# Fewer weight units decoded under attention, raw tiles behind the gates' rows, one gate and val step in two parts

## The chip, the cores and the metric

The kernel runs on one core of one Trainium2 chip. The metric is the device time of one execution in microseconds (us). A profiled execution has a span besides, from its first to its last instruction.

## The reference, cut to what matters

```python
# attention, 2 x 8 heads, 576 positions, 64 dims (8 "pairs" of heads in the kernel)
scores = scale * q @ k.T ; cum = cumsum(max(s, 0))
scores = where(causal, -1e9, scores + min(-(cum_i - cum_j), 0))   # the gates' rows carry cum
x = softmax(scores) @ v                     # [1152, 512]
xn = x / sqrt(mean(x*x) + 1e-6) * rms_g
g, val = xn @ w_gate, xn @ w_val            # [1152, 1536]; the "gate and val" steps
y = (silu(g) * val) @ w_out                 # [1152, 512]
h = y @ w_in ; out = (h * tanh(log(1 + exp(h)))) @ w_out2
```

All inputs arrive as float32 but for the weights, which arrive as 64-bit words.

## The kernel before

Attention runs over eight pairs of heads (p = 0 to 7). A pair has five score units, so there are 40 units, numbered i = 5p + u, and the order of the program is written out by hand: every operation is an event `at(t, f, ...)` whose time t is counted in units, and the events are sorted by t. Each engine and each DMA queue then works through its own instructions in that order, and waits at its head for what the instruction needs.

For pair p+1 the events of pair p load four things. `load_k` and `load_q` (L120, L123, 576 KB each) are issued by POOL at i + 0.2. `load_raw` (L116, two halves of 288 KB, one per head) goes at i + 0.3, on ACT's queue for p below 3 and on SP's from p = 3 on. `load_cum` (L128, L129, four small DMAs of the gates' rows) goes on SP at i + 1.47, and `load_v` (L144) at i + 3.58. Then `q_lo` (L140) and `k_lo` (L134) subtract the rounded q and k from the raw ones: those of the first head on POOL at i + 3.14 and i + 3.28, those of the second on VectorE (DVE) at i + 4.19 and i + 4.89. The first score unit of pair p+1 (PE L391, L392) needs the first head's two.

The weights are 68 units of 512 KB. A unit is loaded by `w_load` (L298) into a tile r and decoded in steps: `w_a` (ACT, L310), `w_b` (two DVE operations, L315 and L317), `w_c` (a copy on ACT, L326, and a subtraction, L328, on POOL during attention and on DVE afterwards). The next load into the same tile waits for the subtraction, and the SP queue is held meanwhile. With `NA = 8` the events decode one unit per pair: `wa` at i + 5.21, `wb` at i + 8.38 and 8.46, `wc` at i + 10.45. So units 0 to 6 are decoded by the end of attention and unit 7 is begun. The first two loads are on ACT's queue, at the times `lim1` (2.19) and `lim8` (8.49). The rest is decoded by `w_tick`, whose event times for the head of the second stage are the list `T["tk"]`; a tick finds the next unit by itself.

After attention comes the head of the second stage, at `to` = 43.83. There `gate_val(0, 0)` to `gate_val(0, 3)` (PE L591, 24 matmuls each, the first twelve with gate weights and the last twelve with val weights) run while the second half of x is normed: `xn_sq` (ACT L516), twelve small DVE operations (`rs_op`, L521 to L531), `xn_scale_t` (ACT L544, five tiles), and the transposes `xn_1` (PE L549). A gate and val step takes one of two PSUM tiles, which `silu` (ACT L598, DVE L599) gives back.

Much later, in the loop over the 36 `y_acc` steps (PE L622), a tick follows each odd k, k = 23 among them, where `y_evac` (L629, L630) also stands. `h_split` (ACT L604, DVE L605) makes the input of the step two ahead.

Of the kernel before, what the change touches and what calls it, by code (L numbers as in the profile page):

```python
# [27 lines left out]
NP = B * H // 2  # L28
# [3 lines left out]
NF, NF2 = DFF // 128, DFF2 // 128  # L32
TB = 384
NB = NTOK // TB
NA = 8
NPRE = 4
KD = DM // 128
KW = 2 * S
# [4 lines left out]
def tile_kernel(ctx: ExitStack, tc: tile.TileContext, kq, qq, v, s, w1, w2, rms_g, out):  # L43
    nc = tc.nc
# [199 lines left out]
    def unit(n):  # L244

        if n < NI:
            return ring_unit(n % 8)
        if n < NU1:
            return w14_unit(n - NI)
        n -= NU1  # L250
        if n < 9:
            return ring_unit((n + 8) % 9)
        if n < 15:
            return slot_unit((0, 5)[n % 2 == 0], (n - 9) // 2)
        if n < 27:
            return w14_unit(n - 15)
        return slot_unit((7, 11)[n // 3 - 9], n % 3)


    gv_done, y_done = set(), set()  # L260
# [74 lines left out]
    def w_tick():  # L335

        n = done["c"]
        if n >= NUW or not free(seq[n]):
            return
        w_loads(LIM[0])  # L340
        done["t"] += 1
        for m in range(done["a"], min(n + 3, done["l"])):
            if m > n and done["t"] - loaded[m] < AGE:
                break
            w_a(m)
            done["a"] = m + 1
        for m in range(done["b"], min(n + 2, done["a"])):
            w_b(m)
            done["b"] = m + 1
        if n < done["b"]:  # L350
            w_c(n)
            done["c"] = n + 1
        w_loads(LIM[0])
# [208 lines left out]
    def banksS():  # L562
        return psS[1].tile([128, 2, 512], F32, tag="S", name="gv")
# [9 lines left out]
    gv_t, h_t, y_t, htile = {}, {}, {}, {}  # L573
# [6 lines left out]
            htile[z] = sbt([128, 8, TB], F32, n, f"h_{n}")  # L580
        return htile[z][:, y]

    def gate_val(b, f):
        t = banksS()
        gv_t[b, f] = t
        for g in range(2):
            n = 0
            w = unit(2 * f + g)
            for c in range(KD):
                for a, r in PASS:  # L590
                    nc.tensor.matmul(t[:, g, 0:TB], w[:, a, 128 * c:128 * c + 128],  # L591
                                     xhl[r][:, c, TB * b:TB * b + TB], start=(n == 0), stop=(n == 11))
                    n += 1
        gv_done.add((b, f))

    def silu(b, f):
        t, h = gv_t.pop((b, f)), h_at(b, f)
# [3 lines left out]
    def h_split(b, f):  # L601
        h = h_at(b, f)
        h_t[b, f] = hhl = sbt([128, 2, TB], F32R, ("hA", "hB", "mm")[(NF * b + f) % 3], "hhl")
        nc.scalar.copy(out=hhl[:, 0], in_=h)  # L604
        nc.vector.tensor_tensor(out=hhl[:, 1], in0=h, in1=hhl[:, 0].bitcast(F32), op=ALU.subtract)  # L605

    def y_acc(b, f):
        if f == 0:
            if b % 2:
                a0, a1 = banksS(), banksS()  # L610
                y_t[b] = [x[:, y, 0:TB] for x in (a0, a1) for y in range(2)]
            else:
                a0 = psT.tile([128, 512], F32, tag="T", name="y0")
                a1 = psT.tile([128, 512], F32, tag="T", name="y1")
                a2 = psT.tile([128, 512], F32, tag="T", name="y2")
                a3 = psX.tile([128, 512], F32, tag="X", name="y3")
                y_t[b] = [x[:, 0:TB] for x in (a0, a1, a2, a3)]
        hhl = h_t.pop((b, f))
        w = unit(NI + f)
        for d in range(KD):  # L620
            for y, (a, r) in enumerate(PASS):
                nc.tensor.matmul(y_t[b][d], w[:, a, 128 * d:128 * d + 128], hhl[:, r],  # L622
                                 start=(f == 0 and y == 0), stop=(f == NF - 1 and y == 2))
        y_done.add((b, f))

    def y_evac(b, ds=range(KD)):
        for d in ds:
            h, l = (x[:, d, TB * b:TB * b + TB] for x in xhl)
            nc.scalar.copy(out=h, in_=y_t[b][d])  # L629
            nc.vector.tensor_tensor(out=l, in0=y_t[b][d], in1=h.bitcast(F32), op=ALU.subtract)  # L630
# [209 lines left out]
    def at(t, f, *args):  # L840
        events.append((t, len(events), f, args))
# [51 lines left out]
    for p in range(NP):  # L893
        i = 5 * p
        z = "z" if p == NP - 1 else ""
        for x in range(2):
            for c, o in enumerate(T[f"av{x}{z}"]):
                at(i + o, av_op, p, x, c)
            at(i + T["xte" + z][x], xt_evac, p, x)
            at(i + T["xtr" + z][x], x_transposes, p, x)  # L900
            at(i + T["xn" + z][x], x_norm, p, x)
        at(i + T["rec" + z], recips, p)
        if NP - NA <= p:
            n = p - NP + NA
            at(i + T["wa"], wa, n)
            if p + 1 < NP:
                at(i + T["wb"][0], wb, n, 0)
                at(i + T["wb"][1], wb, n, 1)
                at(i + T["wc"], wc, n)
        if p + 1 < NP:  # L910
            q1 = nc.scalar if p < 3 else nc.sync
            if p:
                at(i + 0.3, load_raw, p + 1, q1)
                at(i + 0.2, load_k, p + 1)
                at(i + 0.2, load_q, p + 1)
            if p:
                at(i + T["lcum"], load_cum, p + 1)
            at(i + T["lv"], load_v, p + 1, q1)
            los, eng = (T["lo"], T["_le"]) if p else (T["lo0"], T["_l0"])
            for x in range(4):  # L920
                at(i + los[x], (k_lo, q_lo)[x % 2], p + 1, x // 2, nc.vector if eng[x] == "D" else nc.gpsimd)
# [10 lines left out]
    for o, n in ((1.9, 3), (2.05, 2), (3.05, 2), (3.5, 1), (3.95, 2), (4.1, 2)):  # L932
        at(o, busy_x, n)
    at(0.65, q_lo, 0, 1)
    at(T["lim1"], limit, 1, nc.scalar)
    at(T["lim8"], limit, 8, nc.scalar)
    for t in range(5):
        at(T["sq"][t], xn_sq, 0, t)
    for n in range(3):
# [8 lines left out]
    steps1 = [(0, f) for f in range(NPRE)] + [(b, f) for f in range(NPRE) for b in range(1, NB)] + \  # L948
        [(b, f) for f in range(NPRE, NF) for b in range(NB)]
    steps2 = [(b, f) for b in range(NB) for f in range(NF)]  # L950
    to = T["mlp"]
# [1 line left out]
    at(T["limN"], limit, NUW)  # L953
    K0 = len(T["gv"])
    for k in range(K0):
        at(to + T["gv"][k], gate_val, *steps1[k])
        at(to + T["silu"][k], silu, *steps1[k])
    for o in T["tk"]:
        at(to + o, w_tick)
# [12 lines left out]
    for k in range(K0, len(steps1)):  # L972
        gate_val(*steps1[k])
        silu(*steps1[k])
        if k + 1 < len(steps1):
            w_tick()
        if k + 3 >= len(steps1):
            h_split(*steps2[k + 3 - len(steps1)])
    for k, (b, f) in enumerate(steps2):
        if k:  # L980
            w = k + 2
            if w < len(steps2):
                h_split(*steps2[w])
        y_acc(b, f)
        if f == NF - 1 and b < NB - 1:
            y_evac(b)
        if k % 2 == 1:
            w_tick()
    h2_mm(0, 0)
    mlp2.append(True)  # L990
# [110 lines left out]
```

## Time and profile before

| | us |
|---|---|
| median of 3 runs | 543.95 |
| lowest and highest run | 540.23, 544.28 |
| the profiled execution | 543.94 |
| its span | 542.2 |

A PE instruction that waits inside the pipeline can count as busy, so its busy share says little by itself. What the rest of the text reads is where an engine's idle time is noted behind an instruction, in square brackets with the releaser, and which instruction followed which.

### The profile page before, as it was taken

How to read it: one execution, taken by the hardware profiler on the slowest of the kernel's cores; microseconds unless marked ns; L12 is line 12 of the kernel's file. 1: busy time of each engine (PE TensorE's matmuls, PEld its weight loads, DVE VectorE, ACT ScalarE, POOL GpSimd, SP SyncE). 2: the span in 40 equal slices, each digit the busy share in tenths (PEclk: the TensorE clock that was granted, in tenths of full speed). 3: DMA queues.
4: the chain of work that ended last, by engine and by line, in shares of the span. 5: the costliest groups of instructions: out<-in, count | busy, mean ns of one | idle time of the engine just before them, and what ended most of it. 6: DMA issues, size and time to landing. Idle time of an engine off the chain costs nothing.

```text
span 542.2 us, 8007 instructions
## 1 busy us (share of the span) xinstructions
PE 530.3 (98%) x2993; PEld 476.9 (88%) x2993; DVE 339.0 (63%) x718; ACT 265.7 (49%) x594; POOL 56.9 (10%) x67
## 2 busy tenths in 40 slices
PE   8999998999999999999999999999999999999997
PEld 3677775778999999999999999998989999999885
DVE  7989998664635544554567547487678766653321
ACT  5778996677434334433446355555424343333311
POOL 7246455110000000000000000000000000000000
PEclk9999998799999999999999999999999999999999
DMA  9997992203234344434433405344300100000101
GB/s 213 273 246 213 247 244 95 79 8 149 77 94 140 117 119 131 139 116 121 133 100 114 117 1 156 116 117 124 109 0 2 59 1 1 0 1 0 60 0 58
DMA packets 18502, 55.46 MB, mean 102 GB/s; under 512 B 2136, under 2 KB 2392, under 8 KB 18464
## 3 DMA queue, kind: packets, MB, share of 16 engines
q1 hardware_dynamic: 13536, 42.02, 25.1%
q0 software_dynamic: 3488, 9.44, 8.8%
q10 hardware_dynamic: 1440, 3.51, 2.1%
q8 instruction: 23, 0.38, 0.3%
q14 instruction: 15, 0.12, 0.1%
HBM read 52.47 MB, written 2.36 MB: 101 GB/s over the span
## 4 chain that ended last, share of the span: by engine, by line
PE 85%; ACT 6%; DVE 4%; DMA 2%; issue 1%; POOL 0%; ACTq 0%; DVEq 0%; POOLq 0%
PE gv L591 26%; PE o L696 12%; PE y L622 8%; PE gv L646 8%; PE gv L696 6%; PE gv L622 4%; PE xa L477 4%; PE pa L784 3%; PE pc L784 3%; PE pd L784 3%; PE tp L439 3%; ACT px L423 2%; DMA w<-in_qq_dram 2%; PE sc L391 1%; PE pb L784 1%
## 5 line engine op out<-in xcount | busy, mean ns | idle before, releaser
L591 PE MATMUL gv<-xh,wring 128*128 128x384 f32 x576 | 147.8, 337 | 0.0
L591 PEld LDWEIGHTS gv<-xh,wring 128*128 128x128 f32 x576 | 104.0, 188 | 0.1
L591 PE MATMUL gv<-xl,wring 128*128 128x384 f32 x288 | 96.8, 336 | 0.0
L599 DVE TENSOR_TENSOR h_w<-h_w,gv 128x384 f32<-128x384 f32 x36 | 19.9, 554 | 62.4 <-ACT h_w L598 62.4
L598 ACT ACTIVATE h_w<-gv 128x384 f32<-128x384 f32 x36 | 17.7, 491 | 79.5 <-PE gv L591 79.5
L591 PEld LDWEIGHTS gv<-xl,wring 128*128 128x128 f32 x288 | 54.2, 188 | 0.0
L622 PE MATMUL y<-hhl,w 128*128 128x384 f32 x288 | 50.5, 334 | 0.6 <-DVE hhl L605 0.6
L622 PEld LDWEIGHTS y<-hhl,w 128*128 128x128 f32 x288 | 49.9, 188 | 0.9 <-DVE hhl L605 0.9
L317 DVE SCALAR_TENSOR_TENSOR r<-r 128x512 int32<-128x512 int32 x68 | 48.2, 709 | 3.0
L423 ACT ACTIVATE px<-sc,cst 128x384 f32<-128x384 f32 (+2 forms) x80 | 41.3, 531 | 3.6 <-DVE cst L416 3.6
L310 ACT ACTIVATE r<-r 128x512 f32<-128x512 f32 x57 | 38.3, 675 | 2.7 <-DMA r<-in_w_dram 2.1
L416 DVE CUSTOM_DVE_ANT_0 sc<-sc,xtm 128x384 f32<-128x384 f32 (+4 forms) x72 | 34.7, 499 | 4.6 <-PE sc L392 3.2
L605 DVE TENSOR_TENSOR hhl<-h_w,hhl 128x384 fp32r<-128x384 f32 x36 | 19.8, 555 | 24.6 <-ACT hhl L604 24.6
L604 ACT CAST hhl<-h_w 128x384 fp32r<-128x384 f32 x36 | 18.5, 518 | 31.7 <-PE y L622 18.1
L439 PE MATMUL tp<-cst,px 128*128 128x128 f32 (+1 forms) x200 | 31.4, 287 | 2.6 <-ACT aw L458 0.9
L439 PEld LDWEIGHTS tp<-cst,px 128*128 128x128 f32 (+1 forms) x200 | 24.3, 145 | 8.1 <-ACT aw L458 1.1
L477 PE MATMUL xa<-aw,px 128*64 128x320 f32 (+3 forms) x192 | 30.2, 384 | 0.1
L315 DVE TENSOR_SCALAR r<-r 128x512 int32<-128x512 int32 x68 | 29.3, 431 | 0.0
L676 DVE TENSOR_TENSOR glb<-u,glb 128x768 fp32r<-128x768 f32 x20 | 19.1, 955 | 15.9 <-ACT glb L675 15.7
L696 PE MATMUL o<-wt,glb 128*128 128x512 f32 x108 | 26.9, 390 | 0.0
L696 PE MATMUL o<-w,glb 128*128 128x512 f32 x108 | 26.5, 390 | 0.0
L622 PE MATMUL gv<-hhl,w 128*128 128x384 f32 x144 | 25.1, 334 | 0.0
(202 smaller groups left out, 1025.7 us busy)
## 6 DMA issues: line engine op xcount, KB each, us to landing
r<-in_w_dram SPq DMA_DIRECT2D x66, 512.0 KB
w<-in_kq_dram POOLq DMA_DIRECT2D x7, 576.0 KB, 5.5
w<-in_qq_dram POOLq DMA_DIRECT2D x7, 576.0 KB, 6.4
out_dram<-osb SPq DMA_DIRECT2D x8, 256.0 KB
px<-in_v_dram SPq DMA_DIRECT2D x5, 320.0 KB
r<-in_w_dram ACTq DMA_DIRECT2D x2, 512.0 KB
px<-in_v_dram ACTq DMA_DIRECT2D x3, 320.0 KB
raw_hA<-in_kq_dram SPq DMA_DIRECT2D x3, 288.0 KB
```

Of the source, the lines that this page charges most:

```text
L310: nc.scalar.activation(out=top, in_=top, func=ACTF.Prelu, scale=2.0 ** -112, alpha=-2.0 ** 32)
L315: nc.vector.tensor_scalar(out=low, in0=low, scalar1=29, scalar2=None, op0=ALU.logical_shift_right)
L317: nc.vector.scalar_tensor_tensor(out=low, in0=top, scalar=3, in1=low, op0=ALU.logical_shift_left, op1=ALU.bitwise_or)
L416: nc.vector.tensor_tensor_reduce(out=sv, in0=sv, in1=m, scale=-0.125, scalar=first, op0=ALU.add, op1=ALU.min, accum_out=sbias[:, c:c + 1])
L423: nc.scalar.activation(out=pv, in_=sv, func=ACTF.Exp, bias=sbias[:, c + x:c + x + 1], scale=-1.0, accum_out=ssum[:, sc:sc + 1])
L439: nc.tensor.transpose(t[0:rows, o - a:o - a + 128], P[pos[i] % 2][:, o:min(e, o + 128)], ident)
L477: nc.tensor.matmul(o, V[z][0:rows, c, ds], r, start=(c == 0), stop=(c == (1, 4)[part]))
L591: nc.tensor.matmul(t[:, g, 0:TB], w[:, a, 128 * c:128 * c + 128], xhl[r][:, c, TB * b:TB * b + TB], start=(n == 0), stop=(n == 11))
L622: nc.tensor.matmul(y_t[b][d], w[:, a, 128 * d:128 * d + 128], hhl[:, r], start=(f == 0 and y == 0), stop=(f == NF - 1 and y == 2))
L646: nc.tensor.matmul(t[:, x, 0:TB], w[:, a, 128 * c:128 * c + 128], xhl[r][:, c, TB * b:TB * b + TB], start=(n == 0), stop=(n == 11))
L696: nc.tensor.matmul(o_t[b][tt], gl[:, r, x, 128 * tt:128 * tt + 128], w[:, a], start=(g == 0 and x == 0 and y == 0), stop=(g == NG - 1 and ...
L784: nc.tensor.matmul(t, A[a][:, 128 * c:128 * c + 128], B[r][:, c], start=(start and n == 0), stop=(n == 5), skip_group_check=True)
```

## The change

`NA` goes from 8 to 6: one weight unit per pair is decoded from pair 2 on instead of from pair 0 on, so units 0 to 4 are finished in attention and unit 5 is begun. The first two loads of weights move by ten units of time with it. Units 5, 6, 7 and the one after them are then decoded by the ticks that stood there before for units 7 and the one after it; two ticks that did nothing now do work. From p = 3 on `load_raw` stands behind `load_cum`. `gate_val(0, 3)` is issued in two parts: its twelve gate matmuls ahead of the transposes `xn_1(0)`, its twelve val matmuls where the whole step stood. In the loop over `y_acc` the tick of k = 23 moves behind the step k = 24.

```diff
-NA = 8
+NA = 6
-    def gate_val(b, f):
-        t = banksS()
-        gv_t[b, f] = t
-        for g in range(2):
+    def gate_val(b, f, parts=(0, 1)):
+        if 0 in parts:
+            gv_t[b, f] = banksS()
+        t = gv_t[b, f]
+        for g in parts:
             n = 0
             w = unit(2 * f + g)
...
-        gv_done.add((b, f))
+        if 1 in parts:
+            gv_done.add((b, f))
...
-                at(i + 0.3, load_raw, p + 1, q1)
+                at(i + (0.3 if p < 3 else T["lcum"] + 0.01), load_raw, p + 1, q1)
                 at(i + 0.2, load_k, p + 1)
                 at(i + 0.2, load_q, p + 1)
...
-    at(T["lim1"], limit, 1, nc.scalar)
-    at(T["lim8"], limit, 8, nc.scalar)
+    at(T["lim1"] + 5 * (NP - NA), limit, 1, nc.scalar)
+    at(T["lim8"] + 5 * (NP - NA), limit, 8, nc.scalar)
...
     for k in range(K0):
-        at(to + T["gv"][k], gate_val, *steps1[k])
+        if k == NPRE - 1:
+            at(to + T["m1"][0] - 0.01, gate_val, *steps1[k], (0,))
+            at(to + T["gv"][k], gate_val, *steps1[k], (1,))
+        else:
+            at(to + T["gv"][k], gate_val, *steps1[k])
...
-        if k % 2 == 1:
+        if k % 2 == 1 and k != 2 * NF - 1 or k == 2 * NF:
             w_tick()
```

## Rows read from the trace of the kernel before

**Rows 1.** Windows by stage: busy us of each engine, granted clock, DMA share, GB/s.
```profile
core 0: us, PE busy (x) PEld busy (x) DVE busy (x) ACT busy (x) POOL busy (x), PEclk, DMA share, GB/s
44.00:84.00 40.00, 39.64 (x290) 29.37 (x288) 37.34 (x130) 35.45 (x123) 20.86 (x18) 1.00 0.94 242
84.00:92.00 8.00, 5.88 (x40) 3.78 (x41) 7.66 (x17) 5.97 (x17) 6.02 (x6) 0.99 0.15 45
92.00:102.00 10.00, 10.00 (x42) 8.04 (x44) 7.06 (x24) 5.45 (x20) 4.01 (x5) 0.50 0.32 107
137.00:320.00 183.00, 183.00 (x1057) 183.00 (x1057) 98.72 (x183) 76.20 (x144) 0.00 (x0) 1.00 0.38 113
```

**Rows 2.** Timeline of PE (start, us, instruction, [idle before]): first scores of four pairs.
```profile
31.14 0.33 PE L391 MATMUL sc<-w 128*128 128x128 f32 x1
43.19 0.33 PE L391 MATMUL sc<-w 128*128 128x128 f32 x1 [0.50 <-POOL w L134]
65.89 0.33 PE L391 MATMUL sc<-w 128*128 128x128 f32 x1
77.11 0.33 PE L391 MATMUL sc<-w 128*128 128x128 f32 x1
```

**Rows 3.** Timeline of ACT, pair 1: one decode step.
```profile
21.63 0.68 ACT L310 ACTIVATE r<-r 128x512 f32<-128x512 f32 x1
```

**Rows 4.** Timeline of SP's queue, 52 to 72 us.
```profile
52.16 0.42 SPq L116 DMA_DIRECT2D raw_mm<-in_kq_dram  x1
57.95 0.33 SPq L298 DMA_DIRECT2D r<-in_w_dram  x1
60.02 0.47 SPq L129 DMA_DIRECT2D w<-cC  x1
71.56 0.47 SPq L129 DMA_DIRECT2D w<-cC  x1
```

**Rows 5.** Timeline of POOL, pairs 4 and 5.
```profile
62.53 1.42 POOL L140 TENSOR_TENSOR w<-raw_mm,w 64x576 fp32r<-64x576 f32 x1 [4.61 <-issue]
64.03 1.81 POOL L134 TENSOR_TENSOR w<-raw_mm,w 64x576 fp32r<-64x576 f32 x1
66.42 0.72 POOL L123 DMA_DIRECT2D w<-in_qq_dram  x1
72.60 1.88 POOL L140 TENSOR_TENSOR w<-raw_hA,w 64x576 fp32r<-64x576 f32 x1 [3.13 <-issue]
```

**Rows 6.** Timeline of DVE: second head's subtractions for pairs 5 and 6.
```profile
62.77 1.80 DVE L134 TENSOR_TENSOR w<-raw_r,w 64x576 fp32r<-64x576 f32 x1
74.43 0.75 DVE L134 TENSOR_TENSOR w<-raw_hB,w 64x576 fp32r<-64x576 f32 x1
```

**Rows 7.** Timelines of ACT's queue, POOL, SP's queue, ACT: loads, issue and landing.
```profile
20.68 0.33 ACTq L116 DMA_DIRECT2D raw_hA<-in_kq_dram  x1
27.70 1.41 POOL L140 TENSOR_TENSOR w<-raw_hA,w 64x576 fp32r<-64x576 f32 x1 [8.06 <-DMA raw_hA<-in_kq_dram]
324.57 2.93 SPq L298 DMA_DIRECT2D r<-in_w_dram  x2
328.06 0.70 ACT L310 ACTIVATE r<-r 128x512 f32<-128x512 f32 x1 [0.26 <-DMA r<-in_w_dram]
```

**Rows 8.** Timelines of ACT and DVE, head of the second stage.
```profile
121.66 0.63 ACT L516 ACTIVATE w<-w 128x512 f32<-128x512 f32 x1
124.24 0.17 DVE L521 TENSOR_SCALAR cst<-cst 128x5 f32<-128x5 f32 x1 [1.89 <-ACT w L516]
126.79 3.18 ACT L544 ACTIVATE w<-w,cst 128x512 f32<-128x512 f32 x5 [1.87 <-DVE cst L531]
126.61 0.55 DVE L599 TENSOR_TENSOR h_w<-h_w,gv 128x384 f32<-128x384 f32 x1
```

**Rows 9.** Timelines of DVE and PE around the tick of k = 23.
```profile
323.85 0.69 DVE L328 TENSOR_TENSOR wt<-r,wt 128x512 fp32r<-128x512 f32 x1
325.06 1.14 PE L622 MATMUL y<-hhl,w 128*128 128x384 f32 x5 [0.60 <-DVE hhl L605]
```

## The prediction

> **What bounds the kernel now.** I read the windows by stage first, to see where an engine has slack; then the timelines of PE, SP's queue, POOL and DVE through attention, to see what each waits for; then the head of the second stage and the place of the moved tick. In the windows [rows 1] the reader is to see three things. From 137 us on PE is busy all the time, 1057 matmuls in 183 us or 0.173 us each, with DVE and ACT about half idle: work moved there costs nothing as long as it stays off PE's path. From 44 to 84 us nobody has slack: PE 39.64 of 40 us, DVE 37.34, ACT 35.45, and the DMA engines 0.94. And from 92 to 102 us the granted clock is 0.50, the lower of the two levels (1.2 GHz), after a stretch of 8 us in which PE was busy for only 5.88 [rows 1].
>
> The starts of the pairs on PE say what a pair costs [rows 2]: 31.14 to 43.19 is 12.05 us, 43.19 to 65.89 is two pairs of 11.35, 65.89 to 77.11 is 11.22. PE notes one wait there, 0.50 us ahead of pair 3, for POOL's `k_lo` [rows 2]. So about 11.2 us is PE's own pace, and only the first pairs stand above it.
>
> **The change, part by part.** The sum is made against the profiled execution, 543.94 us, which is the median of the runs (543.95) but for 0.01.
>
> *Fewer units under the first pairs.* The chain ahead of pair 2 loses one `w_a` on ACT, 0.68 us long [rows 3], of which I count 0.5, since PE's own work comes up right behind it. Pair 3 starts after a wait of 0.50 for POOL [rows 2]; POOL loses one subtraction, and a later raw load leaves q's transfer freer. Gain 1.0. Bounds: 0, because PE may be the next limit at once, and 1.7, which is what 12.05 + 11.35 - 2 x 11.22 leaves (0.96) plus the 0.68 in pair 1. DVE's and POOL's savings in these pairs beyond that I cost at nothing: PE's pace of 11.2 covers them. Pairs 2 to 6 decode one unit each as before, only with a lower number, so nothing else changes there.
>
> *Raw tiles behind the gates' rows.* This is the part that decides. For pair 5 SP issues raw at 52.16 now, 5.8 us ahead of the weight load at 57.95, which waits for POOL's decode of the unit before; the last gates' row goes at 60.02 [rows 4]. Moved behind it, the two halves go at 60.02 + 0.47 = 60.5 and 61.0. A load of 512 KB on a DMA that is otherwise idle landed 3.5 us after its issue (324.57 to 328.06) [rows 7]. The two halves together hold 576 KB, so by that row the first is there at about 63.4 and the second at 64.0. They are wanted at 62.53 by POOL [rows 5] and at 62.77 by DVE [rows 6]: late by 0.9 and 1.2. Behind DVE's `k_lo` stand the maxima of the last score unit of pair 4, and ACT's exponentials wait for those; behind POOL's two subtractions (62.53 to 65.84 [rows 5]) stands PE's first score matmul at 65.89 [rows 2], which has 0.05 us to spare. I take 1.2. For pair 6 the last row goes at 71.56 [rows 4], so the halves land at 74.9 and 75.5, wanted at 72.60 [rows 5] and 74.43 [rows 6]: late by 2.3 on POOL, where PE has 0.6 to spare (72.60 + 1.88 and the other 1.9 end near 76.5, PE starts at 77.11), and by 1.1 on DVE. Of that the delay that pair 5 already gave is to be taken off on POOL, and I take 1.2 again. Pair 4's raw load meets no weight load ahead of it on SP, because the first two weight loads are on ACT's queue, and pair 7's meets DMA engines with a share of 0.15 [rows 1] and a POOL that has other work to do first: nothing for both. Together a loss of 2.4. Bounds: 0, if the tiles still land in time, because the transfers of k and q have the DMA engines to themselves meanwhile and are out of the way; and 5.0 a pair, 10 in all, if they take the 7.0 us that raw needed in pair 1, issued at 20.68 and awaited until 27.70 among other transfers [rows 7]. I stay near the 3.5 because k and q are issued 6 us or more ahead here (q at 66.42 for a raw load at 72.0 [rows 5]) and 2 us ahead there.
>
> Here the Trainium skill speaks against the change: "DMA: Bandwidth & Descriptors", section "Rules for kernel authors", says to issue a DMA early and wait on it late, so that its fixed cost overlaps with compute; the raw loads do so before and not after. The same page's fit in "Anatomy of one DMA" (2.0 us and the bytes at 436 GB/s) gives 3.35 us for both halves, an estimate from that page; the loss by it would be 1.05 a pair instead of 1.2.
>
> *The head of the second stage.* Two more units are decoded by ticks between the sums of squares (from 121.66) and the twelve small DVE operations (from 124.24) [rows 8]. That is four more ACT instructions of about 0.68 [rows 3], 2.7 us, and one DVE subtraction of 0.69 [rows 9] in series with the last of them: 3.4 us. So the small operations begin at 127.6, end 2.55 later (124.24 to 126.79 [rows 8]) at 130.2, and the five scalings (3.18 [rows 8]) end at 133.4 instead of 129.97. The gate half moved ahead of the transposes gives PE 12 x 0.173 = 2.1 us of work in that time. It can't start at once: it needs the PSUM tile that DVE's L599 gives back, and that stands behind the small operations (126.61 now [rows 8], 130.2 then). Loss between 0 and 3.4 - 2.1 = 1.3; I take 0.6, since the transposes, which now get their tiles one at a time, will find most of them scaled. The new loads are hidden: the tiles are free two decodes ahead, and 3.5 us [rows 7] is less than the 4 us of a gate and val step; without that cover ACT would wait for each.
>
> *The tick of k = 23.* PE waits 0.60 for DVE's L605, which stands behind that tick's decode, the last of it L328 at 323.85 [rows 9]. Moved one step later the decode is behind L605 on DVE. Gain 0.6 (bounds 0 and 0.6); next late would be the load behind the tick, by one subtraction, and its user is a tick that PE doesn't wait for within 2 us.
>
> Sum: -1.0 + 2.4 + 0.6 - 0.6 = +1.4, so 545.3 us.
>
> **The rivals.** *B, the raw loads are hidden after all*, so this part of the change does nothing: -1.0 + 0.6 - 0.6 = -1.0, 542.9 us. For it: both needs are missed by about 1 us only, and without raw k and q land sooner. Against it: DMA engines at 0.94 until 84 us [rows 1].
>
> *C, the clock doesn't fall.* The fall at 92 us follows PE's waits from 84 to 92 us [rows 1], and the order of POOL's and DVE's work there shifts when raw comes later. At the higher level (2.4 GHz) the 10.0 us of PE work would be 5.0, and DVE's 7.06 [rows 1] would be the limit: a gain of 2.9 to 5, and one of the three runs of before was 3.7 below the median. With 3.7 it gives 541.6, with B 539.2. Against it: the operations that made PE wait there are all still in the program. The Trainium skill ("TensorE: Matmul & The Clock Gate", "What's actually happening") has recent activity release the clock; the drop after 5.88 of 8 us agrees.
>
> *D, slower.* The raw tiles come late by 3 us or more per pair, because a second weight load (on ACT's queue, the moved `lim8`) travels with k and q of pair 5. At the bound of 5.0 a pair the sum is -1.0 + 10 + 0.6 - 0.6 = +9.0, 552.9 us. It decides from a landing of 5.3 us on, where two pairs lose 6.
>
> **How the numbers follow.** About 1% (5.4 us) is what a measurement of this kernel can tell from no change. The forecast, 543.9 to 548, has a chance of 0.48; B, 541.5 to 543.9, 0.22; C 0.15; D, 548 to 553, 0.15. Faster by over 1% is below 538.5: C with B and the largest early gain, 0.10. Slower by over 1% is above 549.4: the upper part of D, 0.13. The rest, 0.77, is within 1%. The range of 539.5 to 550 leaves out the ends of C and D.
>
> **What would show it.** Late raw: POOL's first L140 of pairs 5 and 6 waits for a raw tile's DMA, and so does DVE's L134; the first scores of these pairs are 12 us or more apart. Early gain: pair 3 starts without a wait, a microsecond sooner. Head: L521 starts 3 us later after the first gate matmuls than now. Tick: no wait of PE for L605. The prediction is wrong if pairs 5 and 6 keep 11.2 us (B), if the granted clock stays at 1.00 through attention (C), or if it falls a second time.

## The result, and the profile after

The changed kernel takes 547.42 us (median; 543.51 to 555.8), the kernel before 543.45 us on the same chips. The ratio is 1.0064, with an interval of 1.004 to 1.0087: slower by about 3.5 us by the ratio, and by 4.0 by the medians, inside 1%. The ratios here and below leave out the executions that lie over 1.5% above the fastest of their kernel; the medians have them in. Its profiled execution took 548.29 us, with a span of 546.5.

The windows of the changed kernel, with the columns of [rows 1]:

```profile
core 0: us, PE busy (x) PEld busy (x) DVE busy (x) ACT busy (x) POOL busy (x), PEclk, DMA share, GB/s
0.00:20.00 20.00, 17.26 (x63) 9.71 (x63) 12.68 (x34) 9.08 (x26) 12.70 (x27) 0.83 0.94 196
44.00:84.00 40.00, 38.22 (x273) 28.66 (x272) 33.90 (x107) 34.51 (x115) 17.72 (x16) 0.96 0.82 208
92.00:102.00 10.00, 9.04 (x70) 6.83 (x66) 9.69 (x27) 8.07 (x27) 7.53 (x8) 1.00 0.20 50
112.00:137.00 25.00, 22.11 (x128) 19.52 (x128) 12.38 (x35) 15.68 (x34) 2.60 (x2) 0.93 0.48 148
320.00:326.00 6.00, 6.00 (x36) 6.00 (x36) 2.11 (x4) 1.87 (x4) 0.00 (x0) 1.00 0.00 1
```

The fall of the granted clock at 92 to 102 us [rows 1] is gone (1.00), but there are three others: at the start (0.83 over the first 20 us), behind 70 us (0.96 over 40 us), and in the head (0.93 over 25 us). Everything from 44 to 84 us is a little less busy than in [rows 1]. From 320 to 326 us PE is busy throughout.

PE's timeline, first score matmuls of pairs 5 and 6, and the matmuls in the head that waited:

```profile
69.50 0.33 PE L391 MATMUL sc<-w 128*128 128x128 f32 x1 [1.74 <-POOL w L134]
82.35 0.33 PE L391 MATMUL sc<-w 128*128 128x128 f32 x1
131.34 0.44 PE L592 MATMUL gv<-xh,wring 128*128 128x384 f32 x1 [2.15 <-DVE h_w L601]
140.73 0.44 PE L592 MATMUL gv<-xh,wring 128*128 128x384 f32 x1 [0.20 <-DVE h_w L601]
143.14 0.44 PE L592 MATMUL gv<-xh,wring 128*128 128x384 f32 x1 [0.55 <-ACT xh L555]
143.94 0.44 PE L592 MATMUL gv<-xl,wring 128*128 128x384 f32 x1 [0.36 <-DVE xl L556]
```

Against [rows 2], pairs 5 and 6 start 3.61 and 5.24 us later. Pair 5 shows a wait of its own. L592 and L601 are L591 and L599 of before.

SP's queue, POOL and DVE, the raw tiles of pairs 5 and 6 (the answer to [rows 4, 5]):

```profile
61.97 0.47 SPq L129 DMA_DIRECT2D w<-cC  x1
62.49 0.40 SPq L116 DMA_DIRECT2D raw_mm<-in_kq_dram  x1
66.17 1.41 POOL L140 TENSOR_TENSOR w<-raw_mm,w 64x576 fp32r<-64x576 f32 x1 [6.29 <-DMA raw_mm<-in_kq_dram]
79.00 1.41 POOL L140 TENSOR_TENSOR w<-raw_hA,w 64x576 fp32r<-64x576 f32 x1 [5.91 <-DMA raw_hA<-in_kq_dram]
80.48 1.81 POOL L134 TENSOR_TENSOR w<-raw_hA,w 64x576 fp32r<-64x576 f32 x1
66.82 1.37 DVE L134 TENSOR_TENSOR w<-raw_r,w 64x576 fp32r<-64x576 f32 x1 [2.14 <-DMA raw_r<-in_kq_dram]
79.63 1.40 DVE L134 TENSOR_TENSOR w<-raw_hB,w 64x576 fp32r<-64x576 f32 x1 [1.14 <-DMA raw_hB<-in_kq_dram]
```

The raw load stands behind the last gates' row, and POOL now waits for it by name, in pair 5 and in pair 6 (issued at 75.70), and so does DVE for the second halves. In pair 6 POOL's L134 ends at 82.29 and PE begins at 82.35, without a wait of its own: from 71 to 74 us PE was at the lower clock and came late itself.

ACT and DVE in the head (the answer to [rows 8]):

```profile
118.32 0.68 ACT L310 ACTIVATE r<-r 128x512 f32<-128x512 f32 x1 [1.83 <-DMA r<-in_w_dram]
123.34 1.24 ACT L310 ACTIVATE r<-r 128x512 f32<-128x512 f32 x2
127.86 0.69 DVE L328 TENSOR_TENSOR w<-r,w 128x512 fp32r<-128x512 f32 x1 [1.37 <-ACT w L326]
128.47 0.16 DVE L521 TENSOR_SCALAR cst<-cst 128x5 f32<-128x5 f32 x1
130.74 0.55 DVE L601 TENSOR_TENSOR h_w<-h_w,gv 128x384 f32<-128x384 f32 x1
130.92 3.17 ACT L544 ACTIVATE w<-w,cst 128x512 f32<-128x512 f32 x5 [2.70 <-DVE cst L531]
```

Three units, 6, 7 and 8, are decoded here. The first waits 1.83 us for its load, which SP issued at 113.32 and which landed 4.9 us later. The last one's subtraction (127.86) is what the first small operation, L521, stands behind. L601, which gives the PSUM tile back, stands behind the last of the small ones, and PE waits for it at 131.34.

To compare the traces below, I cut each at three places of PE's timeline: from the first matmul of pair 1 (before it the starts differ by up to 4 us) to the first gate matmul, "pairs"; from there to the gate step (1, 0), "head"; from there to the end of the span, "rest".

| trace | units in attention | raw of pairs 4; 5 to 7 | fourth gate | pairs | head | rest | granted clock falls, from pair 1 on |
|---|---|---|---|---|---|---|---|
| before | 8 | early | whole | 95.99 | 21.30 | 405.41 | 92 to 102 |
| after | 6 | late | two parts | 93.45 | 24.62 | 405.77 | 71 to 74, 132 to 136 |
| e2_raw_only | 8 | late | whole | 95.86 | 21.29 | 405.31 | none |
| e5_tick_only | 8 | early | whole | 91.11 | 21.30 | 404.55 | none |
| e12_eight_units | 8 | late | two parts | 96.10 | 20.63 | 406.01 | 72 to 75 |
| e7_gate_whole | 6 | late | whole | 94.31 | 27.62 | 404.33 | 67 to 74, 132 to 139 |
| e10_raw_between | 6 | between; early | two parts | 91.68 | 21.95 | 405.76 | none |

The stretches of before add to 522.70 and those of after to 523.84; the rest of the spans' difference, 3.16 us, lies ahead of pair 1, where the granted clock was 0.83 over the first 20 us in the profile of after and 1.00 in that of before.

The table has one profile of each kernel, and the granted clock differs between executions of one kernel too. It is on record for each execution as a mean. Of the 85 counted executions of the kernel before beside the experiments, the seven with a mean of 1.000 took 539.7 to 540.5 us, and the six with 0.984 took 545.1 to 547.2: some 4 us for 0.01. Over all 85 the mean is 0.992, and over the 19 counted ones of the changed kernel it is 0.992 too. So falls of the clock move a single profile by more than most of the differences below, but they don't account for the 3.5 us by which the changed kernel is slower.

### The profile page after: what moved, and what is told of

Read it like the earlier page. It is cut to its first block, busy times and chain, and to the rows that moved or that the text cites. A ratio compares the mean times of both kernels' runs of the same rounds, so it can differ in the third digit from the quotient of the medians.

```text
span 546.5 us, 7996 instructions
## 1 busy us (share of the span) xinstructions
PE 531.1 (97%) x2993; PEld 478.2 (87%) x2993; DVE 339.1 (62%) x720; ACT 266.9 (49%) x594; POOL 53.1 (10%) x65
## 4 chain that ended last, share of the span: by engine, by line
PE 82%; DVE 5%; DMA 5%; issue 3%; ACT 2%; POOL 1%; SPq 1%; ACTq 0%; DVEq 0%; POOLq 0%
PE gv L592 25%; PE o L698 12%; PE y L624 9%; PE gv L648 8%; PE gv L698 6%; PE gv L624 5%; PE pa L786 3%; PE pc L786 3%; PE pd L786 3%; PE tp L439 2%; DMA raw_hB<-in_kq_dram 2%; PE xa L477 2%; PE pb L786 1%; PE sc L391 1%; DMA w<-in_qq_dram 1%
## 5 line engine op out<-in xcount | busy, mean ns | idle before, releaser
L592 PE MATMUL gv<-xh,wring 128*128 128x384 f32 x576 | 149.2, 339 | 2.9 <-DVE h_w L601 2.4
L592 PEld LDWEIGHTS gv<-xh,wring 128*128 128x128 f32 x576 | 104.9, 189 | 3.8 <-DVE h_w L601 2.8
L592 PE MATMUL gv<-xl,wring 128*128 128x384 f32 x288 | 97.3, 338 | 0.4 <-DVE xl L556 0.4
L601 DVE TENSOR_TENSOR h_w<-h_w,gv 128x384 f32<-128x384 f32 x36 | 19.9, 553 | 62.4 <-ACT h_w L600 62.4
L592 PEld LDWEIGHTS gv<-xl,wring 128*128 128x128 f32 x288 | 54.4, 189 | 0.6 <-DVE xl L556 0.6
L391 PE MATMUL sc<-w 128*128 128x384 f32 (+1 forms) x64 | 24.3, 390 | 1.8 <-POOL w L134 1.7
```

Source lines behind the costliest of these rows:

```text
L391: nc.tensor.matmul(o, QA[z][:, qs], KA[z][:, ks], start=(n != 1), stop=False)
```

## The experiments

Theory L: the raw tiles come late from pair 5 on, and the two more units lengthen the head; the lighter first pairs and the tick give back less. Its rivals are told with each run.

**The raw tiles early again, in the changed kernel.**

```diff
-                at(i + (0.3 if p < 3 else T["lcum"] + 0.01), load_raw, p + 1, q1)
+                at(i + 0.3, load_raw, p + 1, q1)
```

> The changed kernel with one part undone: load_raw stands again ahead of the gates' rows (i + 0.3 for every pair). Theory L (the late raw tiles cost about 1.7 us at pair 5 and 1.6 us at pair 6, as the profile of the changed kernel has 12.94 and 12.85 us there against 11.2): about 3.3 us less than the changed kernel, some 544 us, ratio to before near 1.000; pairs 5 and 6 start 11.2 to 11.5 us apart, and POOL's L140 no longer waits for a raw tile in pairs 4 to 7. Rival W (the two weight loads that now travel in pairs 2 and 3 on ACT's queue make the tiles late): the intervals stay near 12.9 and the time near 547. Rival H (the head of the second stage holds all of the loss): 547 as well, with the intervals short.

549.05 us, ratio 1.0135 (1.009 to 1.0181): slower than the changed kernel, where a gain was expected. PE's first matmul of pair 3, POOL, and SP's queue:

```profile
33.77 0.72 POOL L123 DMA_DIRECT2D w<-in_qq_dram  x1
33.76 0.33 SPq L116 DMA_DIRECT2D raw_hA<-in_kq_dram  x1
46.14 1.96 POOL L140 TENSOR_TENSOR w<-raw_mm,w 64x576 fp32r<-64x576 f32 x1 [11.66 <-DMA w<-in_qq_dram]
49.62 0.48 PE L391 MATMUL sc<-w 128*128 128x128 f32 x1 [4.76 <-POOL w L134]
```

In the kernel before, a weight load stood ahead of pair 4's raw tile on SP and held it until 37.37. With six units that load is on ACT's queue. So the raw tile of pair 4 goes at 33.76, in the same microsecond as k and q of pair 3 and, on ACT's queue, the raw tile of pair 3. The q of pair 3 lands 12.4 us after its issue (in the traces with one raw tile beside it 7.0 to 9.6), PE waits 4.76, and the granted clock falls to 0.50 at about 47 to 54 us. Theory L falls as it stood: undoing the move doesn't give its loss back. Pairs 5 and 6 did come 11.5 and 11.2 us apart again.

**The raw tiles late, in the kernel before.**

```diff
-                at(i + 0.3, load_raw, p + 1, q1)
+                at(i + (0.3 if p < 3 else T["lcum"] + 0.01), load_raw, p + 1, q1)
```

> The kernel before with one part of the change alone: load_raw behind load_cum from p = 3 on, eight units still decoded under attention. Theory L: 2.4 to 3.3 us more than before, 546 to 547, with 12 us or more into pairs 5 and 6, and here into pair 4 too, since a weight load stands ahead on SP's queue in pair 3 as well: up to 1.5 us more. Rival W: no loss, 543.5, because the weight loads on ACT's queue stand where they stood.

545.3 us, ratio 1.0067 (1.0037 to 1.0097). PE's first matmuls of pairs 4, 5 and 6:

```profile
56.10 0.33 PE L391 MATMUL sc<-w 128*128 128x128 f32 x1 [0.90 <-POOL w L134]
69.26 0.33 PE L391 MATMUL sc<-w 128*128 128x128 f32 x1 [1.95 <-POOL w L134]
82.52 0.33 PE L391 MATMUL sc<-w 128*128 128x128 f32 x1 [1.94 <-POOL w L134]
```

With eight units the move alone costs what the whole change costs. Its three waits are 4.79 us; "pairs" is 4.75 us longer than in the run with the tick alone, and neither trace has a fall of the clock to blur that. That the two agree so closely is partly chance: the intervals into pairs 2 and 3, whose raw tiles the move doesn't touch, were 1.05 us longer too, and the one into pair 7 was 1.21 shorter.

**Silu ahead of the small operations**, so that PE's 2.15 us at L592 should go; and the same with the raw tiles early.

```diff
-        "silu": (0.95, 2.42, 5.05, 6.38, 8.66, 9.56, 11.87, 12.47),
+        "silu": (0.95, 2.385, 5.05, 6.38, 8.66, 9.56, 11.87, 12.47),
```

> The changed kernel with silu(0, 1) ahead of the twelve small DVE operations (its event time 2.42 becomes 2.385), so that the PSUM tile for the gate matmuls of (0, 3) is free before them. Theory S (PE's wait of 2.15 us for L601 and the fall of the clock behind it come from that order): the gate matmuls start about 2.2 us sooner, the clock stays at 1.00 from 116 to 137 us, 2 to 3.5 us less than the changed kernel, 544 to 545. Rival: the small operations are what the transposes wait for, and they start 0.3 us later; PE waits at the transposes instead, and the gain is under 1 us.

> Both edits at once: load_raw ahead again and silu(0, 1) ahead of the small operations. If L and S both hold and add up: 5 to 6 us less than the changed kernel, 541 to 542, that is 1.5 to 2.5 us less than before: the gain of the lighter first pairs (1.2) and of the moved tick (0.6) is left over. If one of them only moves the loss elsewhere: 544 or more.

548.42 us, ratio 1.0097 (1.0062 to 1.0133), and 554.03 us, 1.0187 (1.0135 to 1.0239). In the first the wait moves: 0.97 and 0.28 us at the transposes instead of 2.15 at L592. Its head is 22.47 us, with no fall of the clock there, 2.15 less than in the changed kernel, but its profile has a fall at 83 to 91 us behind a wait of 2.21 at pair 6, and the runs show no gain. So the runs don't bear out that the time hangs on the order in the head. The second repeats the wait at pair 3 (4.79, q 12.4 us in flight); its profile is of its longest execution (559.16 us), and more isn't read from it.

**The tick alone, in the kernel before.**

```diff
-        if k % 2 == 1:
+        if k % 2 == 1 and k != 2 * NF - 1 or k == 2 * NF:
             w_tick()
```

> The kernel before with the moved tick alone (behind k = 24). The step of the prediction: PE's wait of 0.60 us for L605 goes and nothing comes in its place: 0.6 us less, ratio 0.999, no wait of PE from 320 to 335 us. Rival: the tick's decode or its load is late for the next steps and PE waits elsewhere by as much: ratio 1.000, a new wait of PE behind 326 us.

541.4 us, ratio 0.9961 (0.9927 to 0.9994): faster than both kernels, if by little. Of the 2.1 us about 1 goes with the clock, by an estimate from 4 us for 0.01: the mean over its ten counted executions is 0.995, against 0.992. Its windows:

```profile
92.00:102.00 10.00, 9.74 (x68) 7.09 (x69) 8.53 (x28) 7.68 (x26) 4.00 (x5) 1.00 0.31 105
320.00:326.00 6.00, 6.00 (x37) 6.00 (x36) 5.12 (x11) 3.37 (x8) 0.00 (x0) 1.00 0.53 175
```

The wait for L605 is gone, and "rest" is 0.86 us shorter than before. The clock doesn't fall at 92 us, though nothing of attention was changed: PE has waits of 0.59, 0.90 and 0.67 at 83.6 to 89.8, as before has 0.58, 0.91 and 0.67 at 84.5 to 90.7. So that fall comes and goes with the same program of attention.

**Raw late for pair 4 alone, in the changed kernel.** What e1 showed to be needed is kept, the rest undone.

```diff
-                at(i + (0.3 if p < 3 else T["lcum"] + 0.01), load_raw, p + 1, q1)
+                at(i + (T["lcum"] + 0.01 if p == 3 else 0.3), load_raw, p + 1, q1)
```

> The changed kernel with load_raw behind the gates' rows in pair 3 only, and ahead of them in pairs 4 to 6. Theory L2 (the raw tiles come late only behind a weight load on SP's queue, that is in pairs 4 to 6; in pair 3 no weight load holds the queue, so there raw must stand behind the rows, or it runs with the k and q of the pair before, as it did with raw back everywhere, where q took 12.3 us): no wait of 4.75 us at pair 3, pairs 5 and 6 start 11.2 to 11.6 us apart, about 3 us less than the changed kernel, 544 to 545, and as much as 6 less than with raw back everywhere. Rival W (two weight loads in pairs 2 and 3 load the DMA engines so that raw ahead is late as well): pair 5 or 6 still at 12.5 us or more, no gain.

546.65 us, ratio 1.006 (1.0031 to 1.009): nothing gained. Pair 3 waits 0.24 only, but pair 5 waits 1.37, with the granted clock at 0.50 behind it. POOL, SP's queue and, last, PE's first matmul of pair 6 show the new reason:

```profile
43.77 0.34 SPq L116 DMA_DIRECT2D raw_hA<-in_kq_dram  x1
44.35 0.72 POOL L123 DMA_DIRECT2D w<-in_qq_dram  x1
52.03 1.41 POOL L140 TENSOR_TENSOR w<-raw_hA,w 64x576 fp32r<-64x576 f32 x1 [6.96 <-DMA w<-in_qq_dram]
64.35 1.59 POOL L140 TENSOR_TENSOR w<-raw_mm,w 64x576 fp32r<-64x576 f32 x1 [5.39 <-DMA w<-in_qq_dram]
77.05 1.41 POOL L134 TENSOR_TENSOR w<-raw_hA,w 64x576 fp32r<-64x576 f32 x1
80.78 0.33 PE L391 MATMUL sc<-w 128*128 128x128 f32 x1
```

Pair 4's raw tile now travels with pair 4's k and q (43.72 and 44.35), and q lands 7.7 us after its issue. In the kernel before it had been issued 5.7 us ahead of k, and POOL began 6.1 us after the issue of q (43.71 to 49.83), without a wait for a transfer. A late L134 makes the next k and q late, since POOL issues them behind it; pair 5's q lands at 64.35, and it is q that POOL waits for, not raw.

The last two lines show what the clock alone does: for pair 6 POOL was done at 78.46, 2.3 us ahead of PE, and yet PE took 12.73 us from pair 5 to pair 6, because the clock was at 0.50 from 70 to 73 us.

**The fourth gate and val step whole, in the changed kernel.**

```diff
-        if k == NPRE - 1:
+        if False:
             at(to + T["m1"][0] - 0.01, gate_val, *steps1[k], (0,))
```

> The changed kernel with gate_val(0, 3) whole again, where it stood. If the gate half ahead of the transposes is worth its 2.1 us: PE waits there for the scalings instead, from 128.9 to about 134, and the time is 1 to 2.5 us more than the changed kernel, 548.5 to 550, the clock falling there too. If its start is so late (2.15 us of waiting for L601) that it covers nothing: the same 547, since the transposes then run from 134 on as well and the gate matmuls follow whole.

548.37 us, ratio 1.0106 (1.0071 to 1.0142). PE's waits in the head:

```profile
131.37 0.33 PE L549 MATMUL bank<-cst,w 128*128 128x128 f32 x1 [3.75 <-ACT w L544]
131.98 3.88 PE L549 MATMUL bank<-cst,w 128*128 128x128 f32 x14 [0.28 <-ACT w L544]
```

The two parts do what they are for: 3.75 + 0.28 us of waiting becomes 2.15, and the head 27.62 becomes 24.62. Part of these 3.00 us is the clock, which was low for about 7 us in this head and for 3.4 in that of after. By the runs the two parts gain 0.0042, some 2 us, with intervals that overlap. They cost 1.44 in "rest" (404.33 against 405.77), of which 0.91 are the waits at 143.14 and 143.94; no trace with a whole step has a wait there. The start of this trace has no fall of the clock; six units by themselves don't bring that one.

**Sixteen matmuls on the warm-up tile instead of twelve**, against the fall at the start.

```diff
-    busy(psX.tile([128, 512], F32, tag="X", name="busy"), 12)
+    busy(psX.tile([128, 512], F32, tag="X", name="busy"), 16)
```

> The changed kernel with 16 instead of 12 filler matmuls ahead of the first gates (0.9 us more of them), which fill PE's idle of 0.9 to 1.6 us there. Theory P (the half clock from 9 to 16 us, seen in all four profiles with six units and in neither with eight, comes from that idle and not from the number of units): no fall at 9 to 16 us, pair 1 starts near 20 us instead of 22.5, about 2.5 us less than the changed kernel, 545. Rival: the fall is set by what follows (the wait for q, the first scores), and stays; time 547 to 548.

546.92 us, ratio 1.0065 (1.0031 to 1.0099), as the changed kernel. The profile has no fall at the start, but nor has e7's with twelve: inconclusive for the start, and no gain in the runs.

**Unit 8 behind the second half's scalings.** Theory H against P.

```diff
-    def w_tick():
+    def w_tick(cap=NUW):
...
-        for m in range(done["a"], min(n + 3, done["l"])):
+        for m in range(done["a"], min(n + 3, done["l"], cap)):
...
-        "tk": (-1.55, 0.56, 2.19, 1.55, 2.93, 5.49, 9.64, 8.72, 10.03, 11.95), "q1": (0.61, 1.16, 2.08, 1.75, 2.0),
+        "tk": (-1.55, 0.56, 1.55, 4.6, 4.7, 5.49, 9.64, 8.72, 10.03, 11.95), "q1": (0.61, 1.16, 2.08, 1.75, 2.0),
...
-        at(to + o, w_tick)
+        at(to + o, w_tick, 8 if o < 2 else NUW)
```

> The changed kernel, with weight unit 8 decoded behind the second half's scalings (the head's first three ticks stop at unit 7, the next two come after the scalings) instead of between the first half's square sums. Theory H (the head got longer because three units, 6, 7 and 8, stand on ScalarE and VectorE ahead of the small operations, where before had one): L521 starts about 1.5 to 1.9 us earlier relative to the first gate matmul than in the changed kernel, TensorE's wait of 2.15 us for the second gate activation falls under 0.6, the granted clock stays at 1.00 there, and the time is 1.5 to 3 us below the changed kernel: about 545 us, ratio to the kernel before near 1.002. Theory P (the head is long because of the order on TensorE, the fourth gate in two parts): TensorE waits elsewhere by the same sum, and the ratio stays at 1.006. A third outcome, D: unit 8 is then missed further down, a wait of TensorE at the fifth gate or value step of up to 2 us, and the ratio is 1.006 or more.

548.86 us, ratio 1.0112 (1.0078 to 1.0146): none of the three as told. It is nearest to D, since PE waits further down, but for a PSUM tile and not for unit 8, and longer. DVE and PE:

```profile
124.81 0.17 DVE L521 TENSOR_SCALAR cst<-cst 128x5 f32<-128x5 f32 x1 [1.16 <-ACT w L516]
141.05 0.69 PE L592 MATMUL gv<-xh,wring 128*128 128x384 f32 x1 [5.61 <-DVE h_w L601]
```

L521 is 10.00 us behind the first gate matmul (114.81) instead of 12.36, and PE's 2.15 us are gone: the first half of H holds. But the two ticks behind the scalings now decode three units at a stretch on DVE (135.0 to 140.5), L601 stands behind them, and PE waits 5.61 us, with a fall of the clock after it. The decode is a sum that has to stand somewhere; e9 moved it to a worse place.

**Pair 4's raw tile between two sets of loads.** Theory Q against W.

```diff
-                at(i + (0.3 if p < 3 else T["lcum"] + 0.01), load_raw, p + 1, q1)
+                at(i + (-2.4 if p == 3 else 0.3), load_raw, p + 1, nc.scalar if p == 3 else q1)
```

> The changed kernel, with the raw tile of pair 4 issued on ScalarE's queue in the middle of pair 2, about 38 us (where the kernel before had it by its place behind a weight load on SP: 37.37), and those of pairs 5 to 7 early again. Theory Q (a pair starts when its last key or query transfer lands; raw tiles issued with those transfers delay them, raw tiles issued between two such sets do not; what the first two weight loads did on SP in the kernel before was to put pair 4's raw tile between): pair 3 starts without a wait, pair 4's rows land about 6 us after issue instead of 7.7, pairs 4, 5 and 6 come 11.2 to 11.5 us apart as before, no wait over 0.5 us at their first matmuls, and the time is 3 to 4 us below the changed kernel: 543 to 544.5 us, ratio near 1.000 to 1.002, with the head still long. Rival W (two weight loads on ScalarE's queue are what delays the later pairs): pair 5 still waits 1.3 us or more and the ratio stays near 1.006.

544.31 us, ratio 1.0018 (0.9983 to 1.0054), 0.0046 or 2.5 us below the changed kernel; the intervals of the two overlap a little. ACT's queue, POOL and PE:

```profile
38.51 0.33 ACTq L116 DMA_DIRECT2D raw_hA<-in_kq_dram  x1
44.75 0.71 POOL L123 DMA_DIRECT2D w<-in_qq_dram  x1
50.80 1.42 POOL L140 TENSOR_TENSOR w<-raw_hA,w 64x576 fp32r<-64x576 f32 x1 [5.33 <-DVE cst L416]
59.09 0.63 PE L439 MATMUL tp<-cst,px 128*128 128x128 f32 x4 [1.19 <-DVE w L511]
68.84 0.33 PE L391 MATMUL sc<-w 128*128 128x128 f32 x1
79.96 0.33 PE L391 MATMUL sc<-w 128*128 128x128 f32 x1
128.10 0.44 PE L592 MATMUL gv<-xh,wring 128*128 128x384 f32 x1 [0.95 <-DVE h_w L601]
```

Q holds in the main: no pair waits for its k or q, pairs 3, 4 and 6 start 11.66, 11.13 and 11.12 us after the ones before them; pair 5 takes 12.52, with 1.19 us for DVE inside pair 4, which isn't a transfer's. "pairs" is 91.68, against 93.45. W falls, since the two weight loads stayed on ACT's queue. The head's wait is 0.95 here (its first load landed 3.4 us after its tile came free, not 4.9), the clock stays at 1.00 behind it, and the head takes 21.95.

**Both edits.**

> Both edits: pair 4's raw tile in the middle of pair 2 on ScalarE's queue, those of pairs 5 to 7 early, and unit 8 decoded behind the second half's scalings. If Q and H both hold, their gains add: what is left is the gain of the lighter first pairs (1.0 to 1.2 us) and of the moved tick (0.6 us, 2.0 by the run with the tick alone), and the time is 540 to 542 us, ratio 0.994 to 0.997. If only one of them holds, 543 to 545 us (1.000 to 1.003). If neither, 547 us.

550.35 us, ratio 1.0096 (1.0056 to 1.0136): worse than any outcome that was named. PE and POOL:

```profile
44.20 0.33 PE L391 MATMUL sc<-w 128*128 128x128 f32 x1 [1.47 <-POOL w L134]
40.86 1.40 POOL L140 TENSOR_TENSOR w<-raw_mm,w 64x576 fp32r<-64x576 f32 x1 [8.59 <-DMA w<-in_qq_dram]
```

The wait of e9 is there again (5.60 us at 142.83), and swallows what e10 gained. But Q doesn't hold here as it did in e10: q of pair 3, issued at 31.55, took 9.3 us, and PE waits 1.47 at pair 3 and 0.61 at pair 5. Pair 4's raw tile was issued 4.4 us behind that q here and 5.4 us behind it in e10; whether that makes the difference isn't shown, since q also took 9.6 us in e12, where no raw tile of pair 4 stood there.

**Eight units, all else as changed.**

```diff
-NA = 6
+NA = 8
```

> The changed kernel with eight units decoded in attention again, from pair 0 on; the raw tiles late, the fourth gate in two parts and the tick moved, as in the changed kernel. It stands between the run with the raw tiles alone (ratio 1.0067) and the changed kernel (1.0064). Theory A (six units gain about 1 us in the first pairs and lose more in the head, where three units instead of one are decoded ahead of the small operations): TensorE has no wait over 0.5 us at the second gate activation, from the first gate matmul to the first one of the second half it is 20 to 21.5 us instead of 24.6, and the time is 1 to 3 us below the changed kernel: about 544 us, ratio 1.001 to 1.005. Theory B (six units pay, and the raw tiles alone make the loss): the time is 1 us or more above the changed kernel, 548 us, ratio 1.008 or more. Waits at the first matmuls of pairs 4, 5 and 6 of 0.9, 1.9 and 1.9 us are expected by both, since the raw tiles are late here as there.

545.97 us, ratio 1.0064 (1.0026 to 1.0101), the ratio of the changed kernel: by the runs, six units instead of eight are worth nothing either way, within some 2.4 us (an estimate from the two intervals). Neither theory named that. The trace shows what may cancel. PE and DVE:

```profile
45.02 0.33 PE L391 MATMUL sc<-w 128*128 128x128 f32 x1 [1.89 <-POOL w L134]
57.36 0.33 PE L391 MATMUL sc<-w 128*128 128x128 f32 x1 [1.14 <-POOL w L134]
70.33 0.33 PE L391 MATMUL sc<-w 128*128 128x128 f32 x1 [1.76 <-POOL w L134]
125.31 0.17 DVE L521 TENSOR_SCALAR cst<-cst 128x5 f32<-128x5 f32 x1 [1.89 <-ACT w L516]
```

L521 is 8.75 us behind the first gate matmul (116.56), as before and in e5; the head is 20.63 with no wait, so A's mechanism in the head is as expected, and its time is not. In the pairs it loses 2.65 us against the changed kernel (96.10 against 93.45). Not all of that is the units: at pair 3 it waits 1.89 us, where e2, with the same program of attention, waits 0.51.

## Why the prediction came out right, and where it did not

The time fell into the forecast's band, 543.9 to 548, and the raw tiles are the part that decides, as it said. Its sum was +1.4 us, the runs give +4.0 by the medians and +3.5 by the ratio (whose interval is 2.2 to 4.7). So the direction and the deciding part were right, and the size was not: the sum lies outside the interval, and it is the width of the band that took the result in. The run e10, whose edit touches only the issue of the raw tiles, is 2.5 us below the changed kernel, about the 2.4 that the prediction put for them, though with an uncertainty nearly as large; what is left there is +1.0 us (0.0018), where the other three terms of the sum had -1.0. So it is in those that the sum is likely to have missed. Step by step:

*Raw tiles, +2.4.* The mechanism is right for pair 5: POOL waits by name for the raw tile, and PE for POOL. The flight was taken a little short: 2.9 us from its issue for the first half, 3.0 for the second (and "6 us or more" of distance to q is 5.6 by the prediction's own rows, 66.42 to 72.0); they took 3.7 and 3.9 for pair 5, 3.3 and 3.5 for pair 6. The interval of pair 5 grew by 1.67 us (12.94 against 11.27), where 1.2 was put. That of pair 6 grew by 1.63 (12.85 against 11.22), but there the cause is not separated: in after POOL and PE, the latter slowed by the clock, came to the first score together, and e6 has 12.73 us there with the raw tile early, from the clock alone. That the late tile can cost as much by itself, e2 shows: 1.94 us of wait at pair 6, with the clock at 1.00. In the kernel before, by itself, the move costs 4.75 us in "pairs" (e2 against e5), since pair 4 loses too (0.90 us of wait); by the runs it costs 0.0067, or 3.6 us.

For pairs 4 and 7 the prediction's "nothing" came true (PE has no wait at either, and the intervals are 11.13 and 14.03 us, against 11.43 and 14.68). What it didn't see is why pair 4's tile had to move: it says that pair 4's raw tile "meets no weight load ahead of it on SP", and without that load an early raw tile goes with k and q of pair 3 and costs 4.76 us there (e1). So the move guards against one delay and makes another. In e10, between two sets of loads, it made neither; in e11 a wait of 1.47 at pair 3 came back.

The rule of the Trainium skill that the prediction weighed ("DMA: Bandwidth & Descriptors", "Rules for kernel authors": issue early, wait late) agrees with e2, where late issue cost 0.67%, and not with e1, where the earliest issue cost more than the late one.

*Lighter first pairs, -1.0.* The profile of after shows it, from pair 1 to pair 3: 22.77 us against 23.69. But with eight units e5 took 22.41 there, e2 23.46 and e12 24.56; with six e3, e6, e7, e8, e9 and e10 took 22.33 to 23.08, and e11, with a wait of 1.47 at pair 3, 23.98. Over the whole of "pairs", six units with late raw tiles took 93.45 to 95.29 us (after, e3, e7, e8, e9), eight took 95.86 and 96.10 (e2, e12). The gain is of the predicted size, and not sharper than the spread of one program's traces. (The upper bound of 1.7 is 1.64 by its own two numbers.)

*The head, +0.6.* L521 "starts 3 us later": it did, 12.36 against 8.75 us after the first gate matmul. PE's wait for L601 is there too. Mis-sized were two terms. "The new loads are hidden": ACT waited 1.83 us for the first (4.9 us in flight, not 3.5), and PE 2.15 instead of at most 1.3. And behind that wait the granted clock fell, 132 to 136 us, which no term held. From the first gate matmul on, six units take 427.7 us in e10, with 0.95 us of wait and no fall, and 430.4 in after; eight take 426.6 (e12). So, with one trace each, the decode costs about 1.1 us while the clock holds, and 3.7 with the longer wait and the fall.

*Two parts of the gate.* Right as a cover with six units (e7: +3.00 in the head without it). The prediction gave no price for what the order does afterwards: 1.44 us in "rest", so that with eight units it is a net loss (e12 against e5 from the first gate matmul on: 426.64 against 425.85).

*The tick, -0.6.* Right, and a little over its bound: "rest" is 0.86 shorter in e5, and the wait for L605 is gone in after too.

*The clock.* Two signs were named for it. The granted clock did not stay at 1.00 through attention, as C has it: it fell at 71 to 74 us. And it fell again, at 132 to 136, which the prediction named as a sign of being wrong and had no price for. What C says of 92 us alone did come true in the profile: pair 7 to the first gate matmul took 19.73 us instead of 23.70, 3.97 less, inside C's 2.9 to 5. It didn't make the kernel faster, because other falls stood against it; over the executions the mean granted clock is 0.992 in both kernels. Nor had it to do with the change: e5 has no fall there, with attention untouched, and e11, with six units, has one.

What stays open: what decides whether the clock falls behind a given wait; whether the fall at the start (in after, e1, e3, e4, e6 and e10, in none of the traces with eight units, nor in e7, e8, e9 and e11) has to do with six units; the real size of the early gain; and what of pair 6's delay in the changed kernel is the raw tile's.

## What to carry to other kernels

A load that waits in a queue may be holding the one behind it at a good place; whoever takes it out of the queue has moved the other too, and should look with which transfers it now travels. Decode work taken out of a full stage must be placed again one instruction at a time: ahead of a chain that gives back a buffer it put that chain off by 3.6 us here (L521, 12.36 against 8.75), of which PE waited for 0.95 to 2.15; in one stretch later it cost a wait of 5.61. And where one profile each is compared, cut the traces at common places and see several before a microsecond is put down to an edit: executions of the kernel before lay over 7 us apart, and the granted clock moved with them.

## What the runs showed of the hardware

Transfers of one size were in flight for very different times. A q of 576 KB was there within 6.1 us of its issue with a raw tile ahead of it by 6 us, 7.0 to 9.6 us behind it with one beside it, and 12.4 with two (e1, e4). That the raw tiles beside it are the cause is shown by e1, where they alone were moved; the spread from 7.0 to 9.6 has no cause shown.

The granted clock went to 0.50, the lower level (1.2 GHz), behind PE's waits of 1.74 and 2.15 us in after, and stayed at 1.00 (2.4 GHz) through waits of 1.95 and 1.94 in e2 and 1.89 in e12, though 1.76 in the same trace of e12 brought it down. The Trainium skill ("TensorE: Matmul & The Clock Gate", "What's actually happening") ties the clock to recent activity; the falls looked at here stood behind waits, which agrees, but equal waits didn't do the same.
